# A state-space scan taken over pairs of times, and an inverse transform on sums and differences of spectrum halves

## The chip, the cores and the metric

The kernel runs on one core of a Trainium2 chip. The metric is the time of one execution in microseconds (us) of device time; the median of several runs counts. A profile is one execution taken by the hardware profiler; its times are counted from the start of its span.

## What is computed

The inputs are x, k and v of 2048 times by 1024 channels in bf16. The output mixes two results by a gate, `g * a + (1 - g) * b`.

```
g = sigmoid((x * gate_w).sum(-1))
# a: diagonal complex state space, 1024 states
Lam = Lambda_re + 1j*Lambda_im;  Lam_bar = exp(exp(log_dt) * Lam)
Bu = x @ (((Lam_bar - 1)/Lam)[:, None] * (B_re + 1j*B_im)).T
h[t] = Lam_bar * h[t-1] + Bu[t]
a = 2 * real(h @ C.T) + x * Dskip
# b: gated long convolution
ks[t] = sum over 4 taps of k[t-i] * shift_k[i];  kv = ks * v
b = x * (causal_convolution(kv, ssm_k) + kv * ssm_D)
```

## The kernel before

The helpers `mm`, `tt`, `ts`, `act`, `load_t`, `move` and `gather` (lines 94 to 124) put every instruction behind the one before on its engine, so the order on TensorE, VectorE (DVE), ScalarE (ACT), and the DMA queues of SyncE (SP) and GpSimd (POOL) is the order in which the Python code runs. All instructions of the helpers show line 91. Generators with `yield` interleave the steps.

**First stage, b.** Channels are done in eight chunks of 128; the loop of line 881 runs c from 0 to 6, and lines 950 to 979 do the end of chunk 7. In turn c the kernel does the inverse transform of chunk c-1, forms the products of chunk c, transforms chunk c+1, and applies the four taps to chunk c+2. The 2048 times are four blocks of 512; a block is transformed at 512 frequencies.

- `fwd_K` and `fwd_V` (550, 570) multiply by cosine and sine tables on TensorE (tiles `psk`, `psv`); ACT copies the results to SBUF as the spectra `Kh` (or `BT`, a weight tile used as room) and `Vh`.
- `products` (583) multiplies and adds spectra on VectorE block by block; the sums of the blocks gather in `G`; one of the partial sums is added by a DMA (`gather`).
- `inverse` (626) multiplies four frequency tiles of `G` with the tables `CI` and `SI` for four tiles of times, 32 matmuls of 512 columns a chunk (tile `psz`). ACT copies to `cv`, and SP writes that to a scratch in DRAM, from which the second stage reads rows of 128 times (`pbb`).
- `turn_table` (398) makes, for one of eight groups of 128 states, the cosines and sines of the state's turn at 512 times (`TCS`), and the same times the factor of B_bar (`TCSi`): eight or nine ACT instructions and two DMAs that add (`hr`, `TCSi`), or two VectorE instructions for the last two groups.

**Second stage, a.** The times are four blocks of 512 (tb) and the states four pairs of groups (g): 16 steps.

- `Bu(tb, g)` (685): 32 matmuls of 512 columns into two PSUM tiles `bu`; ACT copies each to `U` with one instruction of 1024 columns. Three of the 16 calls stand in the first stage's end, lines 966 to 978; the rest are placed by the loops of lines 1025 and 1033.
- `scan(tb, g)` (696): VectorE turns U by `TCSi` (A, trn), runs four scans of 512 times with the real decay `rv` (W), and turns back by `TCS` (hb).
- `Cy(tb, tl)` (789): 32 matmuls of 512 columns with C (tiles `CT`, loaded transposed) give 128 rows of the output in `psy`; they need hb of all four g. ACT scales them by the gate (`scale_a`, 783).
- `gate_products`, `gate_sum`, `scale_b` (657, 661, 759) make the gate of a row tile: VectorE writes `gd`, ACT sums it, takes two sigmoids, scales `pbb` and writes `gd` again, which a DMA adds to `pbb`. `gd` has one buffer. `finish` (795) multiplies by x, adds and writes out.

PSUM is one pool of four tiles (`ps2`, 83), each two banks.

## Time and profile before

| what | value |
|---|---|
| runs | 416.28, 414.3 and 423.17 us, median 416.28 |
| profiled execution | span 409.4 us from the first to the last instruction |
| median less that span | 6.9 us |
| granted TensorE clock | 1.000 |
| first stage, up to the first instruction of scan 0 | 0 to 194.5 us |
| second stage | 194.5 to 409.4 us |

The whole time of the profiled execution is not listed beside its span; what lies around the span is taken as the difference to the median. A row of the list of groups gives engine, operation, `output<-inputs` by the names of tiles, sizes and count, then busy time in us and the mean ns of one instruction, then the idle time ahead of them with what ended it. Mean durations of one engine overlap, since an engine starts the next instruction ahead of the end of the last: a TensorE matmul of 512 columns has a mean of 379 ns, and 32 in a row take 6.91 us.

### The profile page before, as it was taken

How to read it: one execution, taken by the hardware profiler on the slowest of the kernel's cores; microseconds unless marked ns; L12 is line 12 of the kernel's file. 1: busy time of each engine (PE TensorE's matmuls, PEld its weight loads, DVE VectorE, ACT ScalarE, POOL GpSimd, SP SyncE). 2: the span in 40 equal slices, each digit the busy share in tenths (PEclk: the TensorE clock that was granted, in tenths of full speed). 3: DMA queues.
4: the chain of work that ended last, by engine and by line, in shares of the span. 5: the costliest groups of instructions: out<-in, count | busy, mean ns of one | idle time of the engine just before them, and what ended most of it. 6: DMA issues, size and time to landing. Idle time of an engine off the chain costs nothing.

```text
span 409.4 us, 6010 instructions
## 1 busy us (share of the span) xinstructions
PE 400.9 (98%) x2313; PEld 198.6 (49%) x2313; DVE 398.8 (97%) x472; ACT 264.2 (65%) x335; POOL 58.9 (14%) x81
## 2 busy tenths in 40 slices
PE   7999999999999999999999999999999999999996
PEld 4556455555646464444444434444444444444442
DVE  8899999999999999999999999999999999999995
ACT  5898979999999999987333615255633564477001
POOL 3011110303030302001000000011001110123100
PEclk9999999999999999999999999999999999999999
DMA  7776998999989999969699991434964666498404
GB/s 156 155 153 163 198 184 201 182 134 193 142 179 95 174 187 215 229 130 196 144 233 190 159 184 26 103 73 96 159 162 103 129 156 154 77 206 171 85 28 155
DMA packets 127582, 62.01 MB, mean 151 GB/s; under 512 B 106169, under 2 KB 113089, under 8 KB 127554
## 3 DMA queue, kind: packets, MB, share of 16 engines
q1 hardware_dynamic: 117808, 42.48, 50.7%
q0 software_dynamic: 9664, 19.14, 29.4%
q8 instruction: 18, 0.29, 0.4%
q14 instruction: 10, 0.08, 0.1%
q10 hardware_dynamic: 82, 0.02, 0.0%
HBM read 13.13 MB, written 8.39 MB: 53 GB/s over the span
## 4 chain that ended last, share of the span: by engine, by line
PE 61%; DVE 28%; issue 4%; ACT 4%; DMA 1%; SPq 1%; DVEq 0%
PE psy L91 26%; PE bu L91 13%; PE psk L91 7%; DVE wkh L91 6%; PE psz L91 5%; PE taps L91 4%; DVE W L91 4%; DVE BT L91 4%; DVE G L91 4%; DVE t L91 3%; ACT Vh L91 3%; DVE A L91 2%; DVE trn L91 2%; PE psv L91 2%; DVE hb L91 2%
## 5 line engine op out<-in xcount | busy, mean ns | idle before, releaser
L91 PE MATMUL psy<-CT,hb 128*128 128x512 bf16 x512 | 112.3, 379 | 0.5 <-DVE hb L91 0.5
L91 PE MATMUL bu<-xT,BT 128*128 128x512 bf16 x512 | 112.3, 379 | 0.0
L91 PEld LDWEIGHTS <-BT 128*128 128x128 bf16 x512 | 50.1, 98 | 60.4
L91 PEld LDWEIGHTS <-hb 128*128 128x128 bf16 x512 | 49.8, 98 | 60.9 <-DVE hb L91 1.4
L91 DVE TENSOR_TENSOR_SCAN W<-rv,init,A 128x512 bf16<-128x512 f32 x48 | 57.8, 1263 | 0.0
L91 ACT ACTIVATE U<-bu 128x1024 bf16<-128x1024 f32 x32 | 31.9, 1016 | 27.3 <-PE bu L91 27.2
L91 PE MATMUL psz<-G,SI 128*128 128x512 bf16 x128 | 48.5, 379 | 0.2
L91 PE MATMUL psz<-G,CI 128*128 128x512 bf16 x128 | 48.5, 379 | 0.0
L91 ACT ACTIVATE ga<-psy,gcols 128x1024 bf16<-128x1024 f32 x8 | 8.9, 1114 | 39.2 <-PE psy L91 39.2
L91 PE MATMUL taps<-dg,kT 128*128 128x128 bf16 x512 | 30.3, 219 | 0.8 <-DMA kT<-in_B_k_dram 0.8
L91 ACT ACTIVATE Vh<-psv 128x1024 bf16<-128x1024 f32 x32 | 30.3, 1040 | 0.0
L91 PEld LDWEIGHTS <-kT 128*128 128x128 bf16 x512 | 28.8, 98 | 2.0 <-DMA kT<-in_B_k_dram 1.3
L91 POOL DMA_DIRECT2D pbb<-gd x12 | 10.3, 857 | 132.9 <-ACT gd L91 132.9
L91 PE MATMUL psk<-eok,CF 128*128 128x512 bf16 (+1 forms) x96 | 25.7, 361 | 0.4 <-ACT eok L91 0.4
L91 ACT ACTIVATE BT<-psy,gcols 128x1024 bf16<-128x1024 f32 x5 | 5.6, 1110 | 29.2 <-PE psy L91 29.2
L91 PE MATMUL psk<-eok,SF 128*128 128x512 bf16 (+1 forms) x96 | 24.2, 361 | 0.0
L91 PEld LDWEIGHTS <-SF 128*128 128x128 bf16 x160 | 15.6, 98 | 16.0 <-issue 0.6
L91 PEld LDWEIGHTS <-CF 128*128 128x128 bf16 x160 | 15.3, 98 | 14.4
L91 DVE TENSOR_TENSOR wkh<-BT,Vh 128x3072 bf16<-128x3072 bf16 (+4 forms) x20 | 21.8, 1111 | 0.0
L91 DVE TENSOR_TENSOR wkh<-Kh,Vh 128x3072 bf16<-128x3072 bf16 (+2 forms) x16 | 21.3, 1352 | 0.0
L91 DVE TENSOR_TENSOR hb<-hb,trn 128x1024 bf16<-128x1024 bf16 (+1 forms) x34 | 20.8, 653 | 0.1
L91 ACT ACTIVATE cv<-psz 128x1024 bf16<-128x1024 f32 x16 | 16.4, 1032 | 6.7 <-PE psz L91 5.9
(156 smaller groups left out, 666.5 us busy)
## 6 DMA issues: line engine op xcount, KB each, us to landing
G<-wkh POOLq DMA_DIRECT2D x6, 768.0 KB, 6.9
cv_scr<-cv SPq DMA_DIRECT2D x16, 256.0 KB, 5.7
v<-in_B_v_dram SPq DMA_DIRECT2D x3, 1024.0 KB
pbb<-cv_scr SPq DMA_DIRECT2D x12, 256.0 KB, 3.1
xr<-in_A_x_dram SPq DMA_DIRECT2D x12, 256.0 KB, 4.4
pbb<-gd POOLq DMA_DIRECT2D x12, 256.0 KB, 3.3
TCSi<-m POOLq DMA_DIRECT2D x8, 256.0 KB, 9.0
ga<-xr POOLq DMA_DIRECT2D x8, 256.0 KB, 3.3
```

What stands on the lines that cost most here:

```text
L91: i = f(*a, **kw)
```

## The change

1. **Scan over pairs.** x is loaded with the 256 even times of a block ahead of its 256 odd times. `Bu` makes the inputs of the odd times first (a = 1), ACT copies them to `U[:, 1]`, then those of the even times (a = 0) in the other half of the same PSUM tile; matmuls with diagonal matrices of Lam_bar (`lamd`) add Lam_bar times the odd input one time earlier, with one column taken from the block before (`ends`). ACT copies that to `U[:, 0]`. The scan runs over 256 even times with the squared decay. VectorE then makes the odd states from the even ones: four scalings (`q`) and three adds into `U[:, 1]`. `Cy` reads even times from hb and odd times from U.
2. **The factor of B_bar moves into C.** `TCSi` goes; `turn_C` scales each CT by a complex column: two ACT instructions of 1024 columns (`m`), two of VectorE on CT in place, one DMA of 512 KB that adds m. The turn table has 256 times and is made for two groups at a time, in turns 1 to 4.
3. **Inverse on sums and differences.** The 512 frequencies are now 1, 5, 9 and so on. `products` ends with two more VectorE instructions of 2048 elements: the sum and the difference of the lower and upper half of the spectrum. `inverse` uses one for the odd and one for the even times: 16 matmuls a chunk. Row tiles of the output are every second time.
4. **Order.** Calls of `Bu` are numbered 0 to 15 by a list. Calls 0 to 3 stand in turns 3 to 6 of the first stage, 4 and 5 at its end; the weights B and x are loaded earlier for that. In the second stage a list `on_pe` sets which `Bu` and `Cy` follow which scan, and the gate's steps and `turn_C` stand between them.

```diff
-            t0 = tb * TB + h * 256
-            load_t(xTs[tb][:, :, h * 256:(h + 1) * 256], xf[t0:t0 + 256, :])
+            load_t(xTs[tb][:, :, h * HB:(h + 1) * HB], xf[tb * TB + h:(tb + 1) * TB:2, :])
...
-        tt(G[:, 0], G[:, 0], t2[:, 1], ALU.subtract)
-        tt(G[:, 1], G[:, 1], t2[:, 0], ALU.add)
+        tt(t2[:, 1], G[:, 0], t2[:, 1], ALU.subtract)
+        tt(t2[:, 0], G[:, 1], t2[:, 0], ALU.add)
...
+        tt(to[:, 1], lo, hi, ALU.add)
+        tt(to[:, 0], lo, hi, ALU.subtract)
...
-                for fi in range(NFI):
+                for fi in range(2):
...
+    order = [(0, 0), (0, 1), (1, 0), (1, 1), (2, 0), (2, 1), (0, 2), (0, 3), (1, 2), (1, 3), (2, 2), (2, 3)]
+    order += [(NTB - 1, g) for g in range(NG)]
...
         for j in range(2):
-            ps = ps2([128, 2, TB], "bu")
-            for c in range(2):
-                for dt_ in range(ND):
-                    mm(ps[:, c], BT[g][:, c, dt_, j * 128:(j + 1) * 128], xT[:, dt_, :], dt_ == 0, dt_ == ND - 1)
-            act(U[:, :, j, :], ps, func=ACT.Copy)
+            ps = ps2([128, 2, 2, HB], "bu")
+            d = lamd[g][:, j]
+            for a in (1, 0):
+                for c in range(2):
+                    for dt_ in range(ND):
+                        mm(ps[:, a, c], BT[g][:, c, dt_, j * 128:(j + 1) * 128], xT[:, dt_, a * HB:(a + 1) * HB],
+                           dt_ == 0 and (a == 1 or c == 0), a == 1 and dt_ == ND - 1)
+                if a == 1:
+                    act(U[:, 1, :, j], ps[:, 1], func=ACT.Copy)
+                    if j == 1 and tb < NTB - 1:
+                        act(ends[:, tb % 2, g], U[:, 1, :, :, HB - 1], func=ACT.Copy)
+            for k, c, o in ((0, 0, 0), (0, 1, 1), (1, 0, 1), (2, 1, 0)):
+                if tb > 0:
+                    mm(ps[:, 0, o, 0:1], d[:, k], ends[:, 1 - tb % 2, g, c, j:j + 1], False, False)
+                mm(ps[:, 0, o, 1:HB], d[:, k], U[:, 1, c, j, 0:HB - 1], False, k == 2)
+            act(U[:, 0, :, j], ps[:, 0], func=ACT.Copy)
+            yield
...
+            q = [w2([128, 2, 2, HB], BF16, "q") for k in range(2)]
+            for k in range(2):
+                for j in range(js.start, js.stop):
+                    ts(q[k][:, :, j], hbs[tb, g][:, :, j], lam[:, k, 2 * g + j:2 * g + j + 1], None, ALU.mult)
+            o, (q1, q2) = U[:, 1, :, js], [x[:, :, js] for x in q]
+            tt(o, o, q1, ALU.add)
+            tt(o[:, 0], o[:, 0], q2[:, 1], ALU.subtract)
+            tt(o[:, 1], o[:, 1], q2[:, 0], ALU.add)
...
+        if c >= 3:
+            bu = Bu(c - 3)
+            steps(bu, 2)
+            fwd_K(n, (0, 1))
+            run(bu)
+            fwd_K(n, (2, 3))
...
+    def turn_C(pi):
+        m = m_pool.tile([128, 2, D], BF16, name="m")
+        for c in range(2):
+            act(m[:, c], CT[pi][:, 1 - c], func=ACT.Identity, scale=mc2i[:, pi:pi + 1])
+        yield
+        for c, f in enumerate((c2r, mc2r)):
+            ts(CT[pi][:, c], CT[pi][:, c], f[:, pi:pi + 1], None, ALU.mult)
+        gather(CT[pi], m)
...
+    on_pe = ([(Bu_next, i) for i in range(8, 12)] + [(Cy_row, k) for k in range(4)]
+             + [(Bu_next, 12), (Bu_next, 13), (Cy_row, 4), (Bu_next, 14), (Cy_row, 5), (Bu_next, 15)]
+             + [(Cy_row, k) for k in range(6, 12)])
+    at = 0
     step(scans[0])
...
+    for j in range(NS):
...
+        turning = [turn_C(2 * j), turn_C(2 * j + 1)] if j < 4 else []
+        for t in turning:
+            step(t)
+        advance(j)
+        for t in turning:
+            run(t)
+        if j > 0:
+            prepare()
...
+        while at < len(on_pe) and at < (j + 1) * 1.3:
+            f, i = on_pe[at]
+            f(i)
+            at += 1
```

`prepare()` is the gate's ACT part of one row tile, `gate_sum` and `scale_b` together. `Bu_next(i)` runs all of call i.

## The prediction

> **What bounds the kernel now.** First I read the page's shares and slices, then the windows by stage, then the chain of work that ended last.

> ```profile
> PE 400.9 (98%) x2313; PEld 198.6 (49%) x2313; DVE 398.8 (97%) x472; ACT 264.2 (65%) x335; POOL 58.9 (14%) x81
> ...
> PEclk9999999999999999999999999999999999999999
> ```

> TensorE and VectorE are both full over the whole span, at full clock. The windows (length, then busy time of TensorE, weight loads, VectorE, ScalarE, POOL) say the same stage by stage:

> ```profile
> 87.70:108.90 21.20, 21.19 (x150) 11.86 (x150) 21.16 (x19) 20.20 (x28) 4.81 (x6) 1.00 1.10 160
> 108.90:130.20 21.30, 21.22 (x151) 11.73 (x150) 21.09 (x19) 20.42 (x29) 4.80 (x6) 1.00 1.11 151
> 242.00:306.00 64.00, 63.54 (x295) 28.51 (x294) 63.68 (x82) 29.25 (x42) 6.85 (x8) 1.00 0.53 112
> ```

> A turn of the first stage takes 21.2 us on both engines, and ScalarE has 1 us to spare. The chain (start, us, what) shows the price of each block of matmuls, and that the second stage is matmuls end to end:

> ```profile
> 94.99 6.05 PE psk L91 x32
> 101.64 3.69 PE taps L91 x64
> 244.86 6.91 PE bu L91 x32
> 251.77 6.91 PE psy L91 x32
> 307.02 0.78 PE p L91 x32
> ```

> So the sum is TensorE's: its work, and each stretch in which something keeps it waiting. The sum is made against the profiled span of 409.4; the median of the runs, 416.3, is 6.9 above it, and I add 6.9 at the end.

> **TensorE's work.** Rows: 512 columns take 6.91/32 = 0.216 us, 128 columns 3.69/64 = 0.058 (0.056 in another taps row, 3.57 for 64), and from `psk` (16 of 512 and 16 of 384 in 6.05) 384 columns take 0.162. 256 columns lie between, on that line: 0.109 (estimate). One column: 0.78/32 = 0.024 in the gate's row.
> - `psz`: 128 matmuls of 512 fewer, -27.6.
> - A `Bu` has 64 matmuls of 256 (6.98), 8 diagonal ones of 255 (0.87) and, but for tb = 0, 8 of one column (0.2; bounds 0.024 and 0.056 each): 7.85 or 8.05 where it was 6.91. Sixteen calls: +17.4.
> - Net -10.2. [...]

> **VectorE.** The rows give 1.135 for a step of 2048 elements (two `G<-G,BT` in 2.27), 0.60 for 1024. Each chunk gets sum and difference: +2.27. `lamd` adds 12 of 0.18 (12 `dg` in 2.2), the parameters 0.4; the second half of the inverse angles goes, -1.9. In the second stage a step falls from 11.75 (scan 0 to 1: 194.5 to 206.3) to about 8.8, `q` and the odd adds included: scans 4 x 0.58, five of 0.60, six of 512 at 0.36, four scalings of 0.22. There it stops being the bound.

> **ScalarE and a new wait.** The old `Bu` filled both halves of a PSUM tile and was copied out later, beside other matmuls. In the changed program's order of instructions, the first matmul of the a = 0 half waits for ScalarE's count after the copy of the a = 1 half, so nothing covers that copy. What is late: the last matmul drains 0.16 (379 - 216 ns), ScalarE copies 512 columns in 0.61 (the 1024 row's 1.016 less 0.407, the difference of the `fa` and `hr` rows at 1024 and 512), the two hand-overs take 0.03 and 0.04 (eok: fold ends 13.04, copy 13.07 to 14.10, next matmul 14.14). That is 0.84, twice a call, 32 times: 26.9. Bounds: 0.42 (a copy as short as a `dg` of 128 columns, half the drain) to 1.25 (a copy of 1024). I take 0.84, it is nearest to the rows. And whatever stands ahead of the copy in ScalarE's queue now holds TensorE up too. Rows for that, from the timeline of ScalarE (start, us):

> ```profile
> 106.27 3.77 ACT L91 ACTIVATE Vh<-psv 128x1024 bf16<-128x1024 f32 x4
> 109.89 0.66 ACT L91 ACTIVATE hr<-hr 128x512 f32<-128x512 f32 x1
> ...
> 115.80 1.30 ACT L91 ACTIVATE dg<-ident,pcol 128x128 bf16<-128x128 bf16 x4
> 116.97 1.04 ACT L91 ACTIVATE cv<-psz 128x1024 bf16<-128x1024 f32 x1
> ...
> 224.29 1.05 ACT L91 ACTIVATE gd<-gd 128x1024 bf16<-128x1024 bf16 x1
> ...
> 229.17 2.13 ACT L91 ACTIVATE U<-bu 128x1024 bf16<-128x1024 f32 x2
> ```

> A row's gate work takes 4.9 us with a table load (224.3 to 229.2), 3.6 without (245.9 to 249.5); an SBUF instruction of 1024 with a column scale about 1.05.

> **First stage, in order.** VectorE is the bound up to turn 2, since TensorE has 3.5 a turn less and no `Bu` yet: its additions up to then are 3 x 2.27 + 2.2 + 0.4 - 1.9 = 7.5, so turn 3 starts its `psz` at 87.7 + 7.5 = 95.2. TensorE idles 14.4 for it. From turn 3 TensorE is the bound: psz 3.46, mirrors 0.43 and 0.59, psk 6.05, taps 3.69, psv 3.45, together 17.67, and a `Bu` with two waits, 9.53: 27.2 (VectorE 23.4). In turn 4 ScalarE comes late to the first copy: after `Vh` it has three sine steps, four of the new turn table, `cv`, `lo`, four `dg`, `cv`; counted on in the rows above, from the end of `psv`, the copy ends 3.4 after its matmuls, not 0.84: 29.8. Turn 5, without the turn table: 28.4. Turn 6 has no taps: 23.1, and 1.1 for the last `Vh`. Then products(7) on VectorE, 172.8 to 194.5 before: 21.75 - 1.2 (two `hr` go) + 2.27 = 22.8; the inverse of chunk 6 and `Bu` 4 and 5 lie beside it (22.9). Scan 0 can start at 95.2 + 27.2 + 29.8 + 28.4 + 24.2 + 22.8 = 227.6, where it was 194.5.

> **Second stage, from there.** TensorE's work: inverse 3.5, ten `Bu` 80.1, sixteen `Cy` 110.6, gate 1.6, and 4.1 from the last matmul to the end as before: 199.9. Twenty waits of 0.84: 16.8. ScalarE's queue beyond those: six `lamd` ahead of `Bu` 6, +1.0; two `turn_C` (4 x 1.05), waiting for CT1, ahead of `Bu` 8, +2.8; two `turn_C` and the gate of row 0 ahead of `Bu` 10: 0.6 + 4.2 + 4.9 + 0.55 after `Bu` 9, while the a = 1 matmuls take 1.75, so +7.7 over 0.84; the same without table load ahead of `Bu` 11, +6.3; gate work and a `ga` ahead of `Bu` 12 and 14, +2.5 and +2.7. Together 23.0. VectorE waits in turn: its in-place scaling of CT waits for ScalarE's `m`, and `gd` waits for the DMA of the row before, so scan 3 ends near 83 us into the stage, CT6 and CT7 are scaled at 85.5 and their DMA of 512 KB lands at 92 (768 KB of `G` took 6.9; bounds 3.3 and 9.0, the `pbb` and `TCSi` rows). The first `Cy`, due to need them at 84.3, waits 7.7. Loads of CT are in time for this (before, all issued within 27 us). Later scans are ahead of TensorE by 10 us and more. Stage: 199.9 + 16.8 + 23.0 + 7.7 = 247.4.

> Transposed loads: two blocks of x more fall into the first stage (2 MB), eight adding DMAs of 256 KB (`TCSi`, `hr`) leave it; turns get longer too. I take nothing for this; the DMA share of 1.1 in the windows is the cover to watch. Loading every second row I bound by nothing and by the `kn` row's 14.4 us against `xT`'s 6.4 to land, hidden by a turn of 27 in between.

> Sum: 227.6 + 247.4 = 475.0 of span, **482** with 6.9.

> **The rivals.**
> - *TensorE's work alone decides* (the other side): the copies are hidden, VectorE gives way, 409.4 - 10.2 + 6.9 = 406. For it: TensorE is 98% busy. Against: the wait in the program's order; it decides only if the added idle time stays under 10.2, or 0.32 a copy, shorter than any ScalarE row of this size. Chance 0.04; ending within 2% of before (the most a measurement can tell from no change; 408 to 424.6) 0.04.
> - *Only short waits*: ScalarE is never behind, so 3.6 in the first stage, 23.0 and 7.7 drop: 448. For it: ScalarE is busy a third of the second stage. Against: strict order of its queue. Chance 0.22.
> - *The clock falls in the idle stretches*: the first matmuls start cold, three of 512 columns in 1.46 us where three take 0.65 later, and run so from 1.2 to about 3.9; one restart costs 1.35. The longest idle time after that is 1.4 and the clock held. [...] Chance 0.20.
> - *DMA becomes the bound in the first stage*: share 1.18 in turn 5; at 15 us, 497. Chance 0.05.
> - My forecast: 0.45.

> **Numbers.** 482; the range takes in the short waits and the falling clock with their bounds, 444 to 494 (0.87 of the chance). Faster 0.04, same 0.04, slower 0.92.

> **What would show it.** Right: idle TensorE ahead of `bu` released by ScalarE's U, 32 times 0.8 or more, 7 to 9 us ahead of calls 10 and 11; scan 0 near 228; `psy` waiting for the CT DMA; VectorE well under TensorE in the second stage. Wrong: `bu` without idle gaps, scan 0 before 215, or a granted clock under 1.

## The result and the profile after

The changed kernel takes 499.25 us (median of 4 runs, 496.65 to 509.04); the kernel before took 419.73 beside it (414.3 to 423.53). The ratio is 1.206, 95% interval 1.194 to 1.218: slower, and 17 us longer than the 482 that was predicted. Ratios compare the faster runs alone, since some runs of several of these kernels, the profiled one of e1_cover among them, are longer at a lower granted clock (the most in e7_both: 466.19 us at 0.943, where its other three took 439.63 to 444.02 at 0.964 to 0.974). The profiled execution took 498.1 us with a span of 496.1; what lies around the span is 2.0 us, where 6.9 was added.

The page, its lines of shares and of the granted clock:

```profile
PE 417.0 (84%) x2895; PEld 260.2 (52%) x2921; DVE 381.5 (77%) x635; ACT 260.6 (53%) x360; POOL 57.8 (12%) x79
...
PEclk9999899899999999999997977879979889999999
```

TensorE fell from 98% to 84%, and no other engine took its place. The granted clock is no longer full: its mean is 0.94, there are dips in the first stage and a trough in slices 22 to 33. A granted clock under 1 is one of the signs that the prediction itself named for being wrong. The windows (turn 3, turn 4, 63 us early in the second stage, its late part; the last three columns are the granted clock, the busy share of the DMA engines and GB/s):

```profile
96.13:125.04 28.91, 27.43 (x204) 17.73 (x207) 24.63 (x27) 17.50 (x25) 3.96 (x5) 0.94 0.84 159
125.04:156.45 31.41, 27.32 (x204) 18.02 (x205) 23.59 (x21) 21.16 (x32) 3.96 (x5) 0.95 0.75 131
256.00:319.00 63.00, 40.42 (x323) 32.18 (x321) 30.07 (x66) 30.81 (x45) 7.18 (x8) 0.81 0.77 124
423.00:488.00 65.00, 64.68 (x296) 29.49 (x302) 51.15 (x117) 23.62 (x23) 12.19 (x14) 1.00 0.54 122
```

From 256 to 319 TensorE is busy for 40.4 of 63 us, and that at a mean clock of 0.81. The DMA share in turns 3 and 4 is 0.84 and 0.75, where the kernel before had 1.10 and 1.11 in its turns. What TensorE waits for (us in total, times, longest):

```profile
PE bu L93 <- ACT U L93: 51.6, 31, 8.4
PE psz L93 <- DVE G L93: 12.1, 5, 4.0
PE psy L93 <- DMA CT<-m: 5.2, 2, 4.3
```

The first line is the new wait of the a = 0 matmuls for ScalarE's copy of the a = 1 half. The chain through `Bu` 9 and 10 shows the long kind. The last a = 1 matmul of `Bu` 10's first half ends at 283.0, and ScalarE first does two `turn_C` and a gate.

```profile
273.96 4.21 PE bu L93 x40
...
281.81 4.25 ACT m L93 x4
286.06 1.04 ACT gd L93 x2
...
287.12 1.28 ACT L93
...
289.89 1.04 ACT gd L93
290.93 0.49 ACT U L93
...
291.46 5.64 PE bu L93 x40
```

And the 40 matmuls from there to the next wait take 5.64, where the 40 of `Bu` 9 in the first line, at full clock, took 4.21. The timeline of TensorE (start, us, what, idle before) shows 16 equal matmuls of `Bu` 8 after a long and after a short wait, and those of `Bu` 10:

```profile
261.54 3.57 PE L93 MATMUL bu<-xT,BT 128*128 128x256 bf16 x16 [3.57 <-ACT U L93]
...
269.09 1.91 PE L93 MATMUL bu<-xT,BT 128*128 128x256 bf16 x16 [0.69 <-ACT U L93]
...
291.46 3.35 PE L93 MATMUL bu<-xT,BT 128*128 128x256 bf16 x16 [8.43 <-ACT U L93]
```

3.57 against 1.91 is half the clock; the window from 260.31 to 267.14 has a granted clock of 0.50. Eight such stretches cost 1.7 (turn 3), 1.6 (turn 4), 2.7, 1.4 and 2.8 (`Bu` 8, 10, 11), 2.0 (first `Cy`), 1.6 and 2.9 (`Bu` 12, 14), each being its time less that of the same matmuls at full clock: 16.7 us. The clock falls in turns 1 and 2 as well (0.50 from 48.7 to 52.1 and from 72.6 to 76.0), but there VectorE is the bound and TensorE waits for it anyway.

### The profile page after: what moved, and what is told of

Its sections match the earlier page's. It is cut to its first block, busy times and chain, and to the rows that moved or that the text cites. A ratio compares the mean times of both kernels' runs of the same rounds, so it can differ in the third digit from the quotient of the medians.

```text
span 496.1 us, 7384 instructions
## 1 busy us (share of the span) xinstructions
PE 417.0 (84%) x2895; PEld 260.2 (52%) x2921; DVE 381.5 (77%) x635; ACT 260.6 (53%) x360; POOL 57.8 (12%) x79
## 4 chain that ended last, share of the span: by engine, by line
PE 63%; ACT 18%; DVE 7%; SPq 4%; issue 4%; DMA 4%; POOL 0%; DVEq 0%; ACTq 0%; POOLq 0%
PE bu L93 23%; PE psy L93 20%; PE psk L93 8%; PE taps L93 4%; SPq L93 4%; PE psz L93 3%; ACT m L93 3%; ACT U L93 3%; ACT Vh L93 2%; ACT gd L93 2%; DVE t L93 2%; DVE G L93 2%; DMA G<-wkh 2%; PE psv L93 1%; DMA CT<-m 1%
## 5 line engine op out<-in xcount | busy, mean ns | idle before, releaser
L93 PE MATMUL bu<-xT,BT 128*128 128x256 bf16 x1024 | 133.9, 288 | 52.3 <-ACT U L93 51.6
L93 PEld LDWEIGHTS <-BT 128*128 128x128 bf16 x1024 | 105.1, 103 | 76.5 <-issue 57.9
L93 ACT ACTIVATE U<-bu 128x512 bf16<-128x512 f32 x64 | 38.2, 596 | 116.2 <-PE bu L93 116.2
L93 PE MATMUL psy<-CT,hb 128*128 128x512 bf16 x249 | 59.3, 392 | 5.6 <-DMA CT<-m 5.2
L93 PE MATMUL psy<-CT,U 128*128 128x512 bf16 x251 | 56.1, 379 | 0.3
L93 PEld LDWEIGHTS <-hb 128*128 128x128 bf16 x256 | 25.4, 100 | 37.4 <-issue 7.8
L93 PEld LDWEIGHTS <-U 128*128 128x128 bf16 x256 | 25.0, 98 | 30.0
L93 DVE TENSOR_TENSOR_SCAN W<-rv,init,A 128x256 bf16<-128x256 f32 x48 | 32.2, 734 | 0.0
L93 PEld LDWEIGHTS <-SF 128*128 128x128 bf16 x192 | 18.8, 98 | 21.2 <-issue 2.2
L93 PE MATMUL psz<-G,SI 128*128 128x512 bf16 x64 | 26.7, 417 | 0.0
L93 DVE TENSOR_TENSOR U<-U,q 128x512 bf16<-128x512 bf16 (+2 forms) x51 | 23.5, 489 | 0.6
L93 PE MATMUL bu<-U,lamd 128*128 128x255 bf16 x128 | 22.2, 280 | 0.0
```

Source lines behind the costliest of these rows:

```text
L93: i = f(*a, **kw)
```

## The experiments

Theory: the prediction's terms are right (an uncovered copy, ScalarE's queue, VectorE in turns 0 to 2), and the clock that falls in the waits comes on top. Rivals: another cause of the slow matmuls, and a second bound that would come out behind the waits.

### The copy covered (e1_cover)

In outline:

```
xs = [ps2([128, 2, 2, HB], "bu") for a in range(2)]   # was one tile for each j
for a in (1, 0):
    for j in range(2):
        ... 16 matmuls into xs[a][:, j]
    if a == 1: act(U[:, 1] (both j), xs[1]); ends
... diagonal matmuls into xs[0]; act(U[:, 0] (both j), xs[0])
```

> The changed kernel, but each call of Bu takes its two PSUM tiles by time parity instead of by state half: all a = 1 matmuls of both halves j into one tile, one copy of 1024 columns, all a = 0 matmuls into the other tile (3.5 us that need nothing of that copy), then the diagonal matmuls and one more copy. The same matmuls, the same output, the same count of PSUM tiles. Theory (the copy that nothing covers costs the waits, and the long ones cost the clock): the 51.6 us that bu waits for ScalarE's U fall to about 10, only calls 10, 11 and 12 still wait, 2 to 3.5 us each, the granted clock holds there (13 us less of slow matmuls): about 445 us, 437 to 455. Rival (VectorE or the loads set the pace behind those waits): the idle time comes back under another name and the time stays over 475.

Measured: ratio 1.112 (1.099 to 1.126), 458.3 to 473.5 us. The waits of `bu` for ScalarE fell from 31 to three, as said, but to 23.5 us in all, not 10: one of them, in `Bu` 11, is 18.5 long. The gain was some 40 us, not the 54 that lead to 445. The idle time came back partly under another name (VectorE's timeline, then TensorE's, of the profiled execution, which took 473.5):

```profile
289.87 0.69 DVE L93 TENSOR_TENSOR gd<-xr,rows 128x1024 bf16<-128x1024 bf16 x1 [28.35 <-DMA xr<-in_A_x_dram]
```

```profile
323.57 1.87 PE L93 MATMUL psy<-CT,hb 128*128 128x512 bf16 x4 [14.37 <-DMA CT<-m]
```

VectorE's gate product for row 1 stands in the middle of a scan and waits for a load that SP issues behind sixteen transposed loads of C and two of x. The scans and the scaling of the last CT queue up behind it, and TensorE's first `Cy` with them.

### Busy instead of idle (e2_busy, e9_ring_busy)

```
+ for _ in range(FILL[i]): mm(<the other half-step's PSUM tile>, BT.., xT.., True, True)   # ahead of a = 0, j = 0
```

> The changed kernel with 206 matmuls of 512 columns more, into PSUM that is overwritten before anyone reads it, placed where TensorE idles for more than 3 us: 13, 17 and 16 ahead of psz in turns 1 to 3, 15, 15, 37, 31, 25 and 17 in the waits of Bu 1, 8, 10, 11, 12 and 14, 20 ahead of the first Cy. Same output. Theory (an idle stretch of over 3 us lowers the granted clock, and that costs about 16 us): the granted clock is 1.00 throughout, Bu halves after the waits take 4.1 to 4.2 us again and not 5.6 to 7.1, and the time falls by 10 to 16, to about 485, although TensorE does 44 us more work. Rival (the matmuls after a wait are slow for another reason, a port or the transfers of that moment): they stay slow and the time is 499 or more.

Measured: 490.8 us (489.7 to 491.8), ratio 1.188 (1.180 to 1.197): faster by 8, less than the 10 to 16 expected, with 44 us more work. Every a = 0 block behind a filled wait was at full speed, such as that of `Bu` 10, whose wait had been 8.43:

```profile
286.40 1.91 PE L93 MATMUL bu<-xT,BT 128*128 128x256 bf16 x16 [0.45 <-ACT U L93]
...
325.98 1.87 PE L93 MATMUL psy<-CT,hb 128*128 128x512 bf16 x4 [6.55 <-DMA CT<-m]
```

The second line is where the rest went: `Bu` 11 ended 9.3 us earlier than in the changed kernel (309.8 against 319.1), but the CT that the first `Cy` waits for came only 2.8 earlier (325.98 against 328.74). So the first `Cy` waited 6.55, and in that wait the clock fell again: the four matmuls of that line take 1.87, where four at full clock take 1.03 (three times 0.216 from start to start, and 379 ns). To test that, the same was done to e8_ring (below), where CT follows TensorE.

> e8_ring with 179 matmuls of 512 columns more, into PSUM that is overwritten before anyone reads it, in the idle stretches over 3 us (13, 17, 18 ahead of psz in turns 1 to 3; 15, 15, 37, 31, 15, 15 in the waits of Bu 1, 8, 10, 11, 12, 14; 18 ahead of the first Cy). Same output. Theory (e2_busy got back only half of the clock's 16 us because the last CT, late through VectorE's wait for the gate row's load, did not move with TensorE; in e8_ring that wait is gone): slow matmuls in e8_ring's trace sum to some 15 us (2.9 in turns 3 and 4, 6.8 in Bu 8, 10 and 11, 2 in the first Cy, 2.8 in Bu 12 and 14), all of it comes back: 480 us, 476 to 484. Rival (half of it is given back whatever the gate's loads do): 487 us or more.

Measured: 482.2 us (482.0 to 487.6) against e8_ring's 494.7; the spans of the profiled runs differ by 11.6. The same 63 us, in e8_ring and with the work added:

```profile
256.00:319.00 63.00, 40.42 (x322) 32.30 (x320) 33.39 (x75) 30.80 (x45) 7.15 (x8) 0.81 0.78 129
...
256.00:319.00 63.00, 58.12 (x440) 40.73 (x442) 34.78 (x79) 36.14 (x51) 8.00 (x9) 1.00 0.69 129
```

The clock is 1.00, not 0.81. Added work makes the kernel faster, so the slow matmuls come of idleness; that is shown. Of the 15 expected 12 came, all of them in the second stage: scan 0 starts at 234.7 in both profiles. In the first stage the profile has 7.3 us of waiting for the transfer into `ks`, where e8_ring's has 0.4; that this took the other 3 is likely, but not shown.

### Part 3 alone (e3_halves)

```
  kernel before, with: frequencies in order (1, 5, 9, ..), NCF over all, CI and SI of 2 tiles,
+ tt(to[:, 1], lo, hi, ALU.add); tt(to[:, 0], lo, hi, ALU.subtract)     in products
+ 16 matmuls a chunk in inverse (were 32)
```

> The kernel before with the third part of the change alone: even frequencies in order, sum and difference of the spectrum's halves on VectorE, inverse of 16 matmuls a half. Rows of b are put back in order by the loads, in two transfers of half the rows. Same output. Theory (VectorE is as full as TensorE there, so 8 times 2.27 us of sums, less 1.9 for the inverse table, go on the end, and the 27.6 us that TensorE saves turn into idle time): 16 us slower than before, 432 to 440 us, TensorE idle ahead of psz for VectorE's G. Rival (TensorE's work decides): up to 27 us faster, 393 to 405.

Measured: 431.0 us, ratio 1.045 (1.037 to 1.052): 15 to 18 us slower, where the theory had 16. A turn of its first stage (49.30 to 72.79), and TensorE's waits:

```profile
49.30:72.79 23.49, 19.89 (x131) 10.76 (x134) 23.42 (x21) 15.66 (x20) 3.95 (x5) 0.90 0.89 115
```

```profile
PE psz L92 <- DVE G L92: 26.4, 7, 5.4
```

VectorE is busy for 23.42 of 23.49; the 27.6 us that `psz` lost stand there as 26.4 of waiting.

### ScalarE's order, and the gate's ring (e4_gate_last, e6_gate_room)

```
- if j > 0: prepare()          # ahead of the on_pe loop, for j in (1, 2, 6, 8)
+ if late_gate: prepare()      # behind it
```

> The changed kernel with ScalarE's gate work of one row (prepare) issued behind TensorE's calls instead of ahead of them in four turns of the second stage: behind Bu 10, Bu 11, Bu 12 and 13, and Bu 14. Same output. Theory (strict order of ScalarE's queue makes those waits): the wait in Bu 12 falls from 5.95 to 0.7 and that in Bu 14 from 4.12 to 0.7, with them 4.5 us of slow matmuls; in Bu 10 the wait falls by 4 to 5, but there the same work only moves on: Bu 11 waits as long as before, the last two CT are scaled about 4 us later and the first Cy waits 4 us longer. Together 12 to 16 us less, about 485. Rival (the gate's own inputs, VectorE's gd and the transfers, set the pace, not its place in the queue): the waits move to the next call and the time is within 4 us of 499.

Measured: 512.3 us, 13 slower than the changed kernel: the expectation failed. (Of the 14 us between the two profiled spans, 4 lie ahead of scan 0, which this edit leaves alone.) The parts it named moved as said (the wait in `Bu` 10 fell from 8.43 to 3.57, those in `Bu` 12 and 14 to 0.7), but the first `Cy` waited 17 us, not 9, and a later one 9.0 for VectorE's `hb`. The reason stands in VectorE's timeline:

```profile
308.63 0.69 DVE L93 TENSOR_TENSOR gd<-xr,rows 128x1024 bf16<-128x1024 bf16 x1 [17.04 <-DMA pbb<-gd]
```

The one `gd` buffer closes a ring: VectorE's product of a row, ScalarE's gate, the transfer out of `gd`, VectorE's next product; and the scans stand behind that product.

```
- name="gd", bufs=1
+ name="gd", bufs=2
```

> e4_gate_last with two gd buffers instead of one. Same output. Theory (e4_gate_last lost 13 us instead of gaining as much, because VectorE's gate product of the next row waits for the one gd buffer, which is free only after the late gate work and its transfer, 17 us, and the scans behind it set the last CT and the first Cy): VectorE's wait falls from 17 to about 10, the first Cy's from 17 to about 7, the 9.0 wait for hb goes: about 500, 495 to 506. Rival (the loss has to do with where the transfers fall): 508 to 515 as e4_gate_last.

Measured: 492.1 us, ratio 1.193 (1.182 to 1.205): 20 us back. Of these, 7 lie ahead of scan 0, which starts at 233.0 here, at 240.3 in e4_gate_last and at 236.3 in the changed kernel, although the first stage is the same code; the 12.5 behind it are what the theory had, so the ring was the cause of the loss there. VectorE's wait is 11.8, now for the load of the row's x, and the first `Cy` still waits 11.5, not 7.

### The two mends together, with and without the covered copy (e5_rows_early, e7_both, e8_ring)

```
+ if pi == 3: loads(1); loads(2)     # among the CT loads; e5, e7, e8
- if j in (1, 2): loads(j)           # where they stood; e5, e7, e8
+ name="gd", bufs=2                  # e7, e8
```

> e1_cover with the loads of gate rows 1 and 2 issued among those of CT (behind CT3), not behind the transposed loads of the last block of x. Same output. Theory (e1_cover came out 14 to 20 us above what was expected because VectorE, ahead of scan 1's second part, waited 28 us for row 1's x, and with it the scaling of the last CT and the first Cy came late): that wait falls under 10 us, the 18.5 us wait in Bu 11 and the 14.4 us ahead of the first Cy fall to under 5 each: 445 us, 438 to 451. Rival (the gate's chain through its one gd buffer takes over at once): within 5 us of e1_cover's faster runs, 455 to 464.

Measured: 459.2 us, ratio 1.112 (1.101 to 1.124): the rival. The load's 28 us were gone, but VectorE waited 13.42 in the same place, and the first `Cy` 14.38 as before. The profile names no releaser for the 13.42; in e7_both, which differs by the second `gd` buffer alone, that wait is gone, so it was the buffer.

> e5_rows_early with two gd buffers. Same output. Theory (with the copy covered, the second stage is then held only by ScalarE's backlog in Bu 10 and 11): 440 us, 433 to 447, ScalarE's waits 2 to 4 us each there, granted clock nearly 1. Rival (VectorE's scans are the bound of the second stage's start whatever the buffers): as e5_rows_early within 3 us.

Measured: 442.9 us (439.6 to 466.2), ratio 1.072 (1.060 to 1.084), as the theory had it, though the granted clock is 0.97 and other waits than ScalarE's are now the longer ones:

```profile
PE psv L93 <- DMA ks<-lo: 9.6, 2, 6.7
PE psz L93 <- DVE G L93: 9.4, 4, 2.8
PE bu L93 <- ACT U L93: 6.2, 2, 4.0
PE psy L93 <- DMA CT<-m: 6.0, 2, 5.4
```

> The changed kernel with the two mends of e7_both, early loads of the gate rows and two gd buffers, but with its own Bu, so that e7_both against this is the price of the uncovered copy alone. Same output. Theory (in the changed kernel ScalarE's queue, not VectorE's waits for the gate, sets the last CT): 494 us, 490 to 499. Rival (the gate's ring is a cost of its own that the prediction missed): 485 or less.

Measured: 494.7 us (492.5 to 496.0), ratio 1.200 (1.187 to 1.213), as the theory had it. e7_both and e8_ring ran on one chip and differ in `Bu` alone: the uncovered copy, with ScalarE's queue behind it and the clock that falls for it, costs 494.7 - 442.9 = 52 us. Of the 54 between the two profiled spans, 12 lie ahead of scan 0 and 42 behind it. The gate's ring and the late loads together cost the changed kernel 5 or less; they become a bound once the copy is covered, or once the gate's work is put later (e4_gate_last).

### How long an idle stretch (e10_gaps)

e9_ring_busy with fewer added matmuls in each wait.

> e9_ring_busy with fewer of the added matmuls, so that idle stretches of different length are left: about 2.7 in Bu 1, 2.3 in Bu 8, 2.4 in Bu 10, 3.1 in Bu 11, 1.8 in Bu 12, 3.1 in Bu 14, 2.8, 2.4 and 2.0 ahead of psz. Same output. Theory (a stretch over about 3.3 us is needed): no fall of the clock, 480 us as e9_ring_busy. Rival (shorter stretches already lower it, by how they lie against some time grid of the clock's): some of those between 2.3 and 3.1 are followed by slow matmuls and others of the same length are not, those under 2 never; 482 to 490 us.

Measured: 488.5 us (two runs). In TensorE's timeline, 16 matmuls after waits of different length (full clock is 1.91):

```profile
264.15 3.54 PE L93 MATMUL bu<-xT,BT 128*128 128x256 bf16 x16 [2.27 <-ACT U L93]
...
293.06 1.91 PE L93 MATMUL bu<-xT,BT 128*128 128x256 bf16 x16 [2.39 <-ACT U L93]
...
309.28 3.22 PE L93 MATMUL bu<-xT,BT 128*128 128x256 bf16 x16 [3.06 <-ACT U L93]
...
357.98 1.91 PE L93 MATMUL bu<-xT,BT 128*128 128x256 bf16 x16 [1.80 <-ACT U L93]
```

The rival was right: 2.27 brought the clock down and 2.39 did not.

## Why the prediction was wrong, point by point

- *Direction and bound*: right. The kernel became slower. TensorE's waits for ScalarE's copies decide it: 52 us hang on the uncovered copy (e7_both against e8_ring). TensorE's work, 10.2 less by the forecast, decided nothing. The DMA rival's 497 is the nearest number, but by luck: the DMA share fell to 0.84, 0.75 and 0.39 in turns 3 to 5.
- *TensorE's work*: right. 16 matmuls of 256 columns take 1.74 from start to start, 0.109 each; `psz` saves what was said, and e3_halves shows it returning as a wait.
- *VectorE in turns 0 to 2*: right. Turn 3 starts at 96.1 (95.2 forecast).
- *The short wait*: right. From one a = 0 block to the next is 4.87 (269.09 to 273.96); less the work of 4.03 that leaves 0.84.
- *ScalarE's backlog in the second stage*: 26.7 (23.0). `Bu` 6, 8, 10 and 11 are within 0.2 of their terms; `Bu` 12 cost 5.3, not 2.5, for its gate waited on VectorE's product, and `Bu` 14 3.4, not 2.7. The first `Cy` waited 5.2, not 7.7.
- *The turns from 3 on*: 28.9, 31.4, 28.4, 24.2, 23.5 against 27.2, 29.8, 28.4, 24.2, 22.8. The last turn ends at 232.6 (227.6); 3.3 of the 5.0 are the clock in turns 3 and 4, 0.9 the late turn 3, 0.7 the last turn. Scan 0 itself starts only at 236.3, for VectorE waits there for the last `psz`; the prediction's sign was "near 228".
- *The step that failed*: "*The clock falls in the idle stretches*", which was a rival with a chance of 0.20. It belongs in the main sum, since the forecast's own waits make the stretches. Which of them are long enough to bring the clock down was the author's assumption: no run ahead of the prediction shows it, for the longest idle time there, behind the cold start, is 1.4, and the clock held. On that assumption the author put the rival at 490, 8 more for six stretches at 1.35, and the range up to 494 takes it in. The runs showed twice that: eight stretches, 16.7 us, counting those that cost time. The six (turns 1 and 2, `Bu` 8, 10 and 11, the first `Cy`) were the wrong ones too: turns 1 and 2 cost next to nothing (turn 3 starts 0.9 late), for VectorE is the bound there, while turns 3 and 4 and `Bu` 12 and 14 were not among them (turn 4's stretch was 3.30). The price of 1.35 came from one cold start; the eight range from 1.4 to 2.9. Second stage: 247.4 forecast, 263.5 measured; 13.4 of the 16.1 between them are the clock, 3.7 ScalarE, -2.5 the first `Cy`; 1.5 are left without a term.
- *The 6.9 around the span*: it was 2.0 here, and every run on record of the changed kernel and its versions has 1.7 to 2.1 between its time and its own span. The 6.9 set the median of several runs against the span of a faster one. That hid 4.9 of the miss by luck: 475.0 + 21.1 + 2.0 = 498.1.

e9_ring_busy, with the clock held by added work, takes 482.2. It isn't the forecast's kernel (it has the gate's ring mended), but it shows the size: less the 16.7 the profiled 498.1 would be 481.4, an estimate. That both lie at the forecast's 482 is partly luck, since 4.9 of that is the wrong 6.9.

No version beat the kernel before. The best, e7_both, is 7% slower. All of its loss lies in the first stage: scan 0 starts at 222.7 (194.5 before), and from there to the end it takes 215.1, the kernel before 214.9. Part 3 alone costs 15 to 18 us (e3_halves). What the rest would cost without part 3 was not tried.

## What to carry to other kernels

Eight of the waits here cost twice: the wait, and the slow clock after it, 1.4 to 2.9 us each and 16.7 in all. A forecast that puts such waits on TensorE has to price both; the second is part of the same case, not a rival to it. In this kernel the a = 0 matmuls waited for ScalarE's copy out of the other half of their PSUM tile, 31 times; with a tile of their own (e1_cover) the three waits left are those of the diagonal matmuls, which read what is copied. That was worth some 40 us alone and 52 with the gate's ring and the late loads mended. Taking a wait away lets the next ring come out (a single buffer, a load late in a queue): look for what the waiting engine's successors need before you count the whole gain.

## What the runs showed of the hardware

```profile
260.81:264.22 3.41, 1.10 (x5) 0.46 (x5) 1.45 (x4) 3.29 (x4) 1.14 (x1) 1.00 1.21 166
264.22:267.64 3.42, 3.42 (x18) 2.39 (x18) 3.42 (x8) 0.00 (x0) 0.86 (x1) 0.50 1.18 211
...
288.12:291.53 3.41, 2.54 (x12) 1.07 (x11) 3.41 (x8) 3.35 (x7) 0.86 (x1) 1.00 0.95 183
291.53:294.94 3.41, 1.89 (x19) 1.69 (x19) 3.38 (x8) 1.47 (x2) 0.87 (x1) 1.00 0.88 168
```

- Such windows, laid over the changed kernel's trace from 7.7 us to the last matmul, sort cleanly. After each of the ten full-clock windows with TensorE busy for 0.00 to 1.07 us the clock was 0.50; after the others, each with 1.71 or more, it stayed at 1.00. At 0.50 it came back after each of the ten windows with 2.98 us busy or more, and after none of the seven with 2.57 or less.
- In turns 1 and 2 of the changed kernel the fall came after the work had resumed: the `psz` blocks start fast and turn slow at about 48.7 and 72.6, behind waits of 3.19 and 3.97. The first of them:

```profile
48.17 0.39 PE L93 MATMUL psz<-G,CI 128*128 128x512 bf16 x1 [3.19 <-DVE G L93]
48.40 0.38 PE L93 MATMUL psz<-G,SI 128*128 128x512 bf16 x1
48.61 0.56 PE L93 MATMUL psz<-G,CI 128*128 128x512 bf16 x1
48.97 0.63 PE L93 MATMUL psz<-G,SI 128*128 128x512 bf16 x1
```
